# First attention chunk: probabilities' sums on GpSimd, scores issued two heads ahead, later weight splits and key preparation

## The chip, the cores and the metric

The kernel runs on one core of one Trainium2 chip. The metric is the device time of one execution in microseconds (us). The engines are named as in the profile: PE multiplies matrices, PEld is its weight load, DVE is VectorE, ACT is ScalarE, POOL is GpSimd, SP is SyncE, which here only issues transfers. PSUM is the memory that PE writes its results to, SBUF the one that holds everything else.

## The reference

Three parts follow each other, all in fp32.

```python
# 1. attention, q k v: (2, 8, 576, 64), f: (2, 8, 576)
scores = scale * np.matmul(q, k.transpose(0, 1, 3, 2))
cum = np.cumsum(np.log(np.clip(f, 0.0001, 1.0)), axis=-1)
scores = np.where(causal, -1000000000.0, scores + cum[..., :, None] - cum[..., None, :])
attn = np.exp(scores - np.max(scores, axis=-1, keepdims=True))
x = np.matmul(attn / (np.sum(attn, axis=-1, keepdims=True) + 1e-09), v)
# 2. four experts on all 1152 tokens, x: (1152, 512), w1: (4, 512, 1024), w2: (4, 1024, 512)
p = domain_probs / (domain_probs.sum(-1, keepdims=True) + 1e-09)
for e in range(E):
    out += p[:, e:e + 1] * (np.maximum(x @ w1[e], 0.0) @ w2[e])
# 3. an MLP: 512 -> 2048 -> 512
h = out @ w_in
y = (h * (1.0 / (1.0 + np.exp(-1.702 * h)))) @ w_out
```

## The kernel before

**Precision.** Each fp32 operand is held as a rounded part (`hi`: `whi`, `xh`, `qhi`) and a remainder (`lo`: `wlo`, `xl`, `qlo`); a product is three matmuls, hi·hi, lo·hi and hi·lo. So weights, keys, queries and activations each need one rounding instruction and one subtraction. For a weight tile the rounding is on ACT (L72) and the subtraction `wlo` on DVE or POOL (L250). For a pair of heads the keys `ks` are rounded on ACT and their remainders subtracted on DVE for one head and on POOL for the other (L579); the queries are rounded (L69) and subtracted (L597) on POOL.

**Chunks.** Tokens go through attention in chunks. The first is batch 0, queries 0 to 255, one head at a time for eight heads; later ones take two heads at a time. When the chunk's attention output exists, the first layer of the first expert starts on it.

**The first chunk.** `first_step(i)` issues step i of twelve; `in_turn` ties the instructions of the steps to the written order on PE, DVE, ACT and POOL. For head h the stages are: scores on PE (L660) into PSUM; mask and maximum on DVE (L690); exponential and sum on ACT (L706); sum plus 1e-9 and reciprocal on DVE (L713, L714); normalisation on POOL (L716); transposes on PE (L818); a copy to SBUF (`first_copy`, L828, on DVE, that of head 7 on ACT); per pair of heads the product with the values on PE (`emit_pv`, L772), then `xh` on ACT and `xl` on DVE (L783, `emit_x2`). `emit_first(k)` (L979) is the first layer for the 128 features that head pair k yields: 4 groups g of 3 matmuls. `turn(FILL[i])` issues dummy matmuls of 128x512 (L1199) whose result nobody reads. Beside that the steps issue the splits of the first weights ("a" from step 2, "b" from step 6, one tile a step, four tiles each), and the keys and queries of the next pair of heads (steps 7 and 9).

**After the first chunk** a scheduler that simulates the engines places the rest: attention of the later chunks between units of the first layer (L958) and of the second (L1127; its results leave PSUM on DVE by `acc`, L1169 and L1171, which needs the probabilities `dpn`). Loads all go through SP's queue in one order (L78), and a load that overwrites a buffer waits in that queue for the buffer's last reader.

**Probabilities.** The table `dpraw` is loaded third; six DVE instructions make `dpn` of it (L461 to L466), ahead of the first maximum:

```python
        tc.keep_in_program_order(nc.vector.tensor_add(s, v[:, 0], v[:, 1]))
        for e in (2, 3):
            nc.vector.tensor_add(s, s, v[:, e])
        nc.vector.tensor_scalar(out=s, in0=s, scalar1=1e-9, scalar2=None, op0=ALU.add)
        nc.vector.reciprocal(out=s, in_=s)
        nc.vector.tensor_mul(out, v, s.unsqueeze(1).to_broadcast([128, 4, NTILE]))
```

Of the kernel before, what the change touches and what calls it, by code (L numbers as in the profile page):

```python
# [18 lines left out]
SA = 256  # L19
# [14 lines left out]
NTILE = NT // 128  # L34
NBLK = 12
NMOE = 8
WARM, FILL = 11, (4, 3, 3, 2, 2, 2, 3, 3,)


class Halves:  # L40
# [11 lines left out]
def attn_moe_mlp(ctx: ExitStack, tc: tile.TileContext, qk0, qk1, qk2, v0, vp, fg, dp, wa_moe, wb_moe, wa_mlp, wb_mlp, out):  # L52
# [176 lines left out]
    def split_w(kind, v_, g):  # L229
        while (kind, v_, g) not in raw_w:  # L230
            next(cv_gen[0])
            load_owed()
        raw = raw_w.pop((kind, v_, g))
        p = wa_p if kind == "a" else wb_p
        if kind == "b" and v_ in (v_exp, v_exp + 2):
            hi, lo = (t[:, g].rearrange("p (a c) -> p a c", a=4) for t in tsr)
        else:
            hi = p.tile([128, 4, 128], F32R, tag="hi", name="whi")
            lo = p.tile([128, 4, 128], F32R, tag="lo", name="wlo")
        hf = hi.rearrange("p a c -> p (a c)")  # L240
        lf = lo.rearrange("p a c -> p (a c)")
        round_act(hf, raw)
        (wa if kind == "a" else wb)[v_, g] = (hi, lo)
        if kind == "a" and v_ in joint:
            joint_raw[g] = raw

        def rest():
            while pair_due:
                pair_due.pop()()
            (nc.gpsimd if v_ == 0 and kind == 'a' and g < 4 else nc.vector).tensor_sub(lf, raw, f(hf))  # L250
            if g % 2:
                if kind == "a" and v_ in joint and v_ not in placed:
                    sum_weights(v_, g // 2)
                pair_due.append(load_pair)

        lo_due.append(rest)
        lo_of.append((kind, v_, g))
# [195 lines left out]
        load(raw, dp)  # L453
        return raw

    def make_probabilities(raw):

        out = const.tile([128, 4, NTILE], F32, name="dpn")
        s = const.tile([128, NTILE], F32, name="dps")
        v = raw.rearrange("p (j e) -> p e j", e=4)  # L460
        tc.keep_in_program_order(nc.vector.tensor_add(s, v[:, 0], v[:, 1]))  # L461
        for e in (2, 3):
            nc.vector.tensor_add(s, s, v[:, e])
        nc.vector.tensor_scalar(out=s, in0=s, scalar1=1e-9, scalar2=None, op0=ALU.add)
        nc.vector.reciprocal(out=s, in_=s)
        nc.vector.tensor_mul(out, v, s.unsqueeze(1).to_broadcast([128, 4, NTILE]))  # L466
        return out

    def begin_late():
        att_scope.close()  # L470
# [69 lines left out]
    def load_plain_late():  # L540
        for i in (1, 0):
            load(groups[4][i][0:64], qk0[1, 1 - i].rearrange("d (g s) -> d g s", g=4))
        load_plain_values(0)
        load_pair()
        load_pair()
        load_plain_values(4)

    def load_heads(p, h0):
# [79 lines left out]
    def emit_scores(c, u):  # L628
# [4 lines left out]
        for q0 in tiles:  # L633
# [13 lines left out]
            for a, z, _ in mm:  # L647
                if plain(c):
                    if q0 == 0:
                        bank = ps_s.tile([128, 512], F32, tag="s", name="s")  # L650
                    pts.append(bank[:, q0:q0 + w])
                else:
                    if not both or not pts:
                        bank = ps_s.tile([128, 512], F32, tag="s", name="s")
                    pts.append(bank[:, 256:256 + w] if both and pts else bank)
                out.append((q0, w, a, z, pts[-1]))
# [163 lines left out]
    def first_copy(h):  # L820

        pt = first_t.pop(h)
        ph = pt_p.tile([128, 4, SB], F32, tag="ph", name="ph").rearrange("p i q -> p (i q)")
        ph_of[0, h] = [ph[:, :SA], ph[:, SA:SA + 128]]
        if h == 7:
            round_act(ph[:, :SA + 128], pt[:, :SA + 128])
        else:
            nc.vector.tensor_copy(ph[:, :SA + 128], pt[:, :SA + 128])  # L828

    def first_step(i):  # L830

        n = len(first_seq)
        p, h0 = passes[1], 0
        prep = [(7, lambda: prep_keys(p, h0, 0)), (7, lambda: prep_keys(p, h0, 1)), (9, lambda: prep_keys(p, h0, 2)),
                (9, lambda: prep_queries(p, h0, 1, (0,))), (9, lambda: prep_queries(p, h0, 1, (1,)))]
        for j in (0, 1) if i == 0 else (i + 1,):
            if j < n:
                emit_scores(*first_seq[j])
        if 3 <= i < n + 3:
            emit_pv(0, i - 3)  # L840
        if i >= 7 and x_used[0] < x_made[0] and x_used[0] < 3:
            emit_first(x_used[0])
            x_used[0] += 1
        if i < n:
            emit_max(*first_seq[i])
            emit_exp(*first_seq[i])
        if 1 <= i <= n:
            emit_norm(*first_seq[i - 1])
        if 2 <= i < n + 2:
            first_copy(i - 2)  # L850
        if 3 <= i < n + 3:
            emit_x2(0, i - 3)
        split_rest()
        for kind, p0 in (("a", 2), ("b", 6)):
            if 0 <= i - p0 < 4:
                split_w(kind, 0, i - p0)
                pass
        for j, fn in prep:
            if i == j:
                fn()  # L860
        if i < len(FILL):
            turn(FILL[i])
        if 1 <= i <= n:
            first_tr(i - 1)
        if i == 0:
            load_cum(p, h0)
        if i == 8:
            load_heads(passes[1], 2)
        if i == 9:
            load_values(p, h0)  # L870

    def attention():
# [16 lines left out]
        for i in range(len(seq) + L_X2 + 1):  # L889
            done = None  # L890
            new = [k for k in nxt if first[k] == i + LEAD]
            new_q = [k for k, j in first_q.items() if j == i + LEAD]
            last_pool = [j for j in nc.cur_bb.bb.instructions if j.engine == nc.gpsimd.engine][-1]
            with tc.issue_after(last_pool) if i == 0 else ExitStack():
                for k in new:
                    prep_parts(*k)
                for k in new_q:
                    prep_queries(*k)
            for k in [k for k in nxt if first[k] == i + 2]:
# [65 lines left out]

    first_p = []

    def emit_first(k, last=False):

        v_, b, c = units[0]  # L970
        for g in range(4):
            if k == 0:
                if g % 2 == 0:
                    first_p.append(ps_tile())
            po = first_p[g // 2][:, SA * (g % 2):SA * (g % 2) + SA]
            whi, wlo = wa[v_, g]
            for j, (w, x) in enumerate([(whi, xh), (wlo, xh), (whi, xl)]):

                nc.tensor.matmul(po, lhsT=w[:, k, :], rhs=x[c][:, k, :],  # L979
                                 start=(k == 0 and j == 0 and g % 2 == 0), stop=(k == 3 and j == 2 and g % 2 == 1))  # L980
# [250 lines left out]
            load_plain_late()  # L1231
    nc.vector.tensor_scalar(out=fr, in0=cum, scalar1=1.0 / NEG, scalar2=None, op0=ALU.mult)
    nc.scalar.dma_start(out=cumd, in_=fr)
    dpn = make_probabilities(dp_raw)
    load_heads(passes[1], 0)
    for _ in range(2):
        load_pair()
# [15 lines left out]
        while ready[0] < c:  # L1253
            pull()

    x_used = [0]
    for i in range(len(first_seq) + 4):
        in_turn(first_step, i)
    ready[0] = 0

    pin_from = [None, 0]
# [115 lines left out]
    late_by = [3]  # L1377
    rest_gen, rest_from = [], seq.index((1,) + units[6])
    cv_due = [0]
    in_turn(emit_first, 3, True)  # L1380
    for i, (kind, v_, b, c) in enumerate(seq):
        if kind == 1 and c < NCH:
            drain(c)
# [161 lines left out]
```

## Time and profile before

| what | value |
|---|---|
| time, median of 3 runs (lowest, highest) | 687.27 us (686.98, 688.13) |
| time of the profiled execution | 687.52 us |
| its span, first to last instruction | 685.8 us |
| PE busy | 676.4 us |
| DVE busy | 531.0 us |
| ACT busy | 353.6 us |
| POOL busy | 244.7 us |
| mean granted TensorE clock | 0.999 |

The profile is of one execution. Its own time is 1.7 us more than its span, which is what lies outside the first and the last instruction. Starts in the rows below are counted from the start of the span. A row with "x4" stands for four instructions one behind another, its second number for the time from the start of the first to the end of the last. What stands in square brackets at a row's end is idle time ahead of it and what ended that.

### The profile page before, as it was taken

Reading aid. Unit: us, or ns where it says so; the run is one execution under the profiler, and the core shown is the slowest. Engines: PE = TensorE matmul, PEld = TensorE weight load, DVE = VectorE, ACT = ScalarE, POOL = GpSimd, SP = SyncE. Lnnn points to the kernel's source line nnn. Section 1 sums busy time; section 2 is a strip of 40 time slices with the busy share of each in tenths; the row PEclk is TensorE's granted clock in tenths of the full one; section 3 lists DMA queues with packets and bytes.
Section 4 is the critical chain, followed back from the end, with each engine's and each line's share of the span. In section 5 each row is a group of like instructions: output and inputs, shape, how many; then the busy total and the mean of one; then the engine's idle time right before and its main releaser. Section 6 shows DMA issues by size and latency. Waiting matters only on the chain.

```text
span 685.8 us, 11068 instructions
## 1 busy us (share of the span) xinstructions
PE 676.4 (99%) x3921; PEld 596.8 (87%) x3921; DVE 531.0 (77%) x1097; ACT 353.6 (52%) x821; POOL 244.7 (36%) x302
## 2 busy tenths in 40 slices
PE   8998999999999999999999999999999999999997
PEld 4797889889888898898898898898999998998986
DVE  6896767788698778777987879767799989988532
ACT  5768767667633735635336253362447453552420
POOL 6886577463342454543135324132003300120000
PEclk9999999999999999999999999999999999999999
DMA  8796637145232135053531423413332534441012
GB/s 254 232 307 245 232 114 246 27 151 169 93 123 92 38 117 169 32 159 133 170 108 48 153 77 108 127 41 100 119 108 77 168 124 153 141 153 62 1 46 93
DMA packets 41063, 87.59 MB, mean 128 GB/s; under 512 B 3720, under 2 KB 5776, under 8 KB 40752
## 3 DMA queue, kind: packets, MB, share of 16 engines
q1 hardware_dynamic: 40680, 84.75, 38.0%
q0 software_dynamic: 288, 2.10, 0.8%
q8 instruction: 31, 0.51, 0.3%
q14 instruction: 24, 0.20, 0.1%
q10 hardware_dynamic: 40, 0.04, 0.0%
HBM read 73.98 MB, written 12.88 MB: 127 GB/s over the span
## 4 chain that ended last, share of the span: by engine, by line
PE 90%; DVE 4%; POOL 2%; DMA 1%; ACT 1%; issue 1%; SPq 0%; POOLq 0%; DVEq 0%
PE m L1127 41%; PE m L1002 23%; PE m L958 15%; PE s L660 4%; PE x L772 3%; PE t L734 3%; DMA qr<-in_qk_dram 1%; POOL e L716 1%; PE m L1283 1%; DMA dpraw<-in_dp_dram 1%; POOL qlo L597 1%; POOL qhi L69 1%; DVE acc L1171 0%; POOL ks L579 0%; DVE wf L434 0%
## 5 line engine op out<-in xcount | busy, mean ns | idle before, releaser
L1127 PE MATMUL m<-whi,hh 128*128 128x512 f32 x392 | 109.6, 393 | 0.0
L1127 PE MATMUL m<-wlo,hh 128*128 128x512 f32 x392 | 108.3, 391 | 0.0
L1127 PE MATMUL m<-whi,hl 128*128 128x512 f32 x392 | 108.2, 390 | 0.0
L250 DVE TENSOR_TENSOR wlo<-wst,whi 128x512 fp32r<-128x512 f32 x132 | 101.5, 783 | 6.3 <-ACT whi L72 5.8
L1013 POOL TENSOR_TENSOR hl<-jc,hh 128x320 fp32r<-128x320 f32 (+1 forms) x60 | 53.1, 888 | 141.1 <-ACT hh L72 141.0
L72 ACT ACTIVATE whi<-wst 128x512 fp32r<-128x512 f32 x136 | 80.6, 624 | 26.3 <-PE m L1127 14.2
L1127 PEld LDWEIGHTS m<-wlo,hh 128*128 128x128 f32 x392 | 73.3, 188 | 15.5
L1127 PEld LDWEIGHTS m<-whi,hl 128*128 128x128 f32 x392 | 73.4, 188 | 15.2
L1127 PEld LDWEIGHTS m<-whi,hh 128*128 128x128 f32 x392 | 71.9, 188 | 12.5
L271 POOL TENSOR_TENSOR sr<-wst 128x256 f32<-128x256 f32 x20 | 18.1, 903 | 149.4 <-DMA wst<-wm 79.6
L716 POOL TENSOR_SCALAR e<-e,sm 128x128 f32<-128x128 f32 (+4 forms) x72 | 44.9, 636 | 48.3 <-DVE sm L714 31.7
L1011 ACT ACTIVATE jc<-jc 128x320 f32<-128x320 f32 (+1 forms) x60 | 27.1, 451 | 54.6 <-DVE jc L1008 54.2
L1171 DVE SCALAR_TENSOR_TENSOR acc<-m,dpn,acc 128x512 f32<-128x512 f32 x63 | 46.5, 744 | 7.8 <-PE m L1127 7.6
L958 PE MATMUL m<-xh,whi 128*128 128x256 f32 (+2 forms) x256 | 51.1, 315 | 0.3 <-ACT xh L72 0.3
L958 PE MATMUL m<-xh,wlo 128*128 128x256 f32 (+2 forms) x256 | 50.6, 313 | 0.0
L958 PE MATMUL m<-xl,whi 128*128 128x256 f32 (+2 forms) x256 | 50.5, 314 | 0.0
L706 ACT ACTIVATE e<-e,mx 128x128 f32<-128x128 f32 (+4 forms) x72 | 41.7, 581 | 10.3 <-DVE mx L690 9.9
L958 PEld LDWEIGHTS m<-xh,whi 128*128 128x128 f32 x256 | 41.2, 189 | 2.2 <-ACT xh L72 0.6
L1110 ACT ACTIVATE m<-m 128x384 f32<-128x384 f32 x48 | 23.0, 479 | 37.1 <-DVE m L1008 35.5
L958 PEld LDWEIGHTS m<-xh,wlo 128*128 128x128 f32 x256 | 41.3, 189 | 0.8
L958 PEld LDWEIGHTS m<-xl,whi 128*128 128x128 f32 x256 | 41.0, 189 | 0.6
L1040 ACT ACTIVATE u<-m 128x320 f32<-128x320 f32 (+2 forms) x26 | 11.2, 432 | 50.5 <-PE m L1002 50.5
(174 smaller groups left out, 1510.1 us busy)
## 6 DMA issues: line engine op xcount, KB each, us to landing
wst<-in_wa_moe_dram SPq DMA_DIRECT2D x28, 512.0 KB, 4.2
wst<-in_wb_moe_dram SPq DMA_DIRECT2D x28, 512.0 KB, 4.3
mst<-in_wa_mlp_dram SPq DMA_DIRECT2D x16, 512.0 KB, 3.7
wm<-wf SPq DMA_DIRECT2D x32, 256.0 KB, 4.0
mst<-in_wb_mlp_dram SPq DMA_DIRECT2D x16, 512.0 KB, 4.2
wst<-wm SPq DMA_DIRECT2D x16, 512.0 KB, 3.9
cb<-cumd SPq DMA_DIRECT2D x16, 256.0 KB, 4.4
qr<-in_qk_dram SPq DMA_DIRECT2D x8, 384.0 KB, 4.6
```

The costliest lines, as they stand in the source:

```text
L72: return nc.scalar.activation(out=out, in_=in_, func=AF.Copy)
L250: (nc.gpsimd if v_ == 0 and kind == 'a' and g < 4 else nc.vector).tensor_sub(lf, raw, f(hf))
L660: nc.tensor.matmul(pt[:, :z - a], lhsT=lr[i][0], rhs=lr[i][1], start=i == 0 and not (both and pt is not bank), stop=i == n - 1, skip_group ...
L706: nc.scalar.activation(out=e[:, off:off + w], in_=e[:, off:off + w], func=AF.Exp, scale=-1.0, bias=mx, accum_out=sm[:, 0, k:k + 1])
L716: nc.gpsimd.tensor_scalar(out=e[:, off:off + w], in0=e[:, off:off + w], scalar1=sm[:, 0, i:i + 1], scalar2=1.0, op0=ALU.mult, op1=ALU.mult)
L958: nc.tensor.matmul(p[:, :n], lhsT=w[:, k, :], rhs=x[c][:, k, :], start=(j == 0 and k == 0), stop=(j == 2 and k == 3))
L1002: nc.tensor.matmul(p[:, :WN], lhsT=w[a][:, k, :], rhs=x[z][:, k, :], start=start and j == 0 and k == 0, stop=stop and j == 2 and k == 1, s ...
L1011: nc.scalar.activation(out=r, in_=r, func=AF.Relu)
L1013: nc.gpsimd.tensor_sub(hl[:, g, :], r, f(hh[:, g, :]))
L1110: nc.scalar.activation(out=p[:, :n], in_=p[:, :n], func=AF.Gelu_apprx_sigmoid)
L1127: nc.tensor.matmul(p, lhsT=h_tile(v_, b, c, j, x, k), rhs=wb[v_, k][w].rearrange("p a c -> p (a c)"), start=i == 0 and k == 0, stop=i == 2 ...
L1171: nc.vector.scalar_tensor_tensor(out=a, in0=p, scalar=d, in1=a, op0=ALU.mult, op1=ALU.add)
```

## The change

All of it is in the code of the first chunk and of what is issued beside it:

- The probabilities' three additions and the 1e-9 go to POOL in step 2, the reciprocal and the product stay on DVE, in step 10.
- Scores are issued two heads ahead instead of one (three heads in step 0), with a third PSUM bank, taken from the pool of the later matmuls. In a step the product with the values comes first, then the transposes, then the scores; the transposes of a head move from the end of one step to the start of the next.
- 11 dummy matmuls instead of 22.
- The weights "a" are split a step later, "b" two steps later; three of the four `wlo` of "a" are on POOL, before all four.
- The copy of head 7 goes from ACT to DVE. The keys and queries of the next pair come in steps 8 and 9. The `emit_first` of pairs 0 to 2 keep a fixed table; the fourth group of each is issued last.
- The rounding of the second pair's keys on ACT is ordered behind the last ACT instruction of the first chunk. On SP two weight loads go ahead of a load of values.

```diff
-WARM, FILL = 11, (4, 3, 3, 2, 2, 2, 3, 3,)
+WARM, FILL = 11, (1, 2, 2, 2, 1, 2, 1)
+X2_AT = {5: 1, 7: 3, 9: 5, 10: 7}
...
-            (nc.gpsimd if v_ == 0 and kind == 'a' and g < 4 else nc.vector).tensor_sub(lf, raw, f(hf))
+            (nc.gpsimd if v_ == 0 and kind == 'a' and g < 3 else nc.vector).tensor_sub(lf, raw, f(hf))
...
+    def sum_probabilities():
+
+        v = dp_raw.rearrange("p (j e) -> p e j", e=4)
+        nc.gpsimd.tensor_add(p_sum, v[:, 0], v[:, 1])
         for e in (2, 3):
...
+            nc.gpsimd.tensor_add(p_sum, p_sum, v[:, e])
+        nc.gpsimd.tensor_scalar(out=p_sum, in0=p_sum, scalar1=1.0, scalar2=1e-9, op0=ALU.mult, op1=ALU.add)
+
+    def make_probabilities():
+
+        nc.vector.reciprocal(out=p_sum, in_=p_sum)
+        nc.vector.tensor_mul(dpn, dp_raw.rearrange("p (j e) -> p e j", e=4), p_sum.unsqueeze(1).to_broadcast([128, 4, NTILE]))
...
-        load_plain_values(0)
         load_pair()
         load_pair()
+        load_plain_values(0)
         load_plain_values(4)
...
-                        bank = ps_s.tile([128, 512], F32, tag="s", name="s")
+                        bank = ps_tile() if hs[0] % 3 == 2 else ps_s.tile([128, 512], F32, tag="s", name="s")
...
-        if h == 7:
-            round_act(ph[:, :SA + 128], pt[:, :SA + 128])
-        else:
-            nc.vector.tensor_copy(ph[:, :SA + 128], pt[:, :SA + 128])
+        nc.vector.tensor_copy(ph[:, :SA + 128], pt[:, :SA + 128])
...
-        prep = [(7, lambda: prep_keys(p, h0, 0)), (7, lambda: prep_keys(p, h0, 1)), (9, lambda: prep_keys(p, h0, 2)),
+        prep = [(8, lambda: prep_keys(p, h0, 0)), (9, lambda: prep_keys(p, h0, 1)), (9, lambda: prep_keys(p, h0, 2)),
                 (9, lambda: prep_queries(p, h0, 1, (0,))), (9, lambda: prep_queries(p, h0, 1, (1,)))]
-        for j in (0, 1) if i == 0 else (i + 1,):
+        if 3 <= i < n + 3:
+            emit_pv(0, i - 3)
+        if 2 <= i < n + 2:
+            first_tr(i - 2)
+        for j in range(3) if i == 0 else (i + 2,):
             if j < n:
                 emit_scores(*first_seq[j])
-        if 3 <= i < n + 3:
-            emit_pv(0, i - 3)
-        if i >= 7 and x_used[0] < x_made[0] and x_used[0] < 3:
-            emit_first(x_used[0])
-            x_used[0] += 1
+        for k, gs in {7: [(0, range(3))], 8: [(1, (0, 1))], 9: [(1, (2,))],
+                      10: [(2, range(3)), (0, (3,)), (1, (3,)), (2, (3,))]}.get(i, ()):
+            emit_first(k, gs)
...
-        if 3 <= i < n + 3:
-            emit_x2(0, i - 3)
-        split_rest()
-        for kind, p0 in (("a", 2), ("b", 6)):
-            if 0 <= i - p0 < 4:
-                split_w(kind, 0, i - p0)
-                pass
+        if i in X2_AT:
+            emit_x2(0, X2_AT[i])
+        if i == 2:
+            sum_probabilities()
+        if i == 10:
+            make_probabilities()
         for j, fn in prep:
             if i == j:
                 fn()
+        if i != 7:
+            split_rest()
+        for kind, p0 in (("a", 3), ("b", 8)):
+            if 0 <= i - p0 < 4:
+                split_w(kind, 0, i - p0)
         if i < len(FILL):
             turn(FILL[i])
-        if 1 <= i <= n:
-            first_tr(i - 1)
...
+                for j in nc.cur_bb.bb.instructions[begin:]:
+                    if i == 0 and j.engine == nc.scalar.engine:
+                        keep_order([first_act[0], j])
...
-    dpn = make_probabilities(dp_raw)
...
+    first_act = [j for j in nc.cur_bb.bb.instructions if j.engine == nc.scalar.engine][-1:]
...
-    in_turn(emit_first, 3, True)
+    in_turn(emit_first, 3, range(4), True)
```

Lines of the changed kernel are a few higher than those of before for the same code: L660 is L663, L690 is L693, L713 is L716, L772 is L775, L818 is L821, L250 is L251, L579 is L582, L1169 is L1177, L1199 is L1207. Three places show how instructions move.

PE's order at the first product with the values (`x<-ph,v`), in steps 2 and 3, before (`t` are transposes, `s` scores, `m<-acc_79` a dummy):

```order
L818 MATMUL t<-identr,e 128x128 x3
L660 MATMUL s<-acc_79 128x128
L660 MATMUL s<-acc_79 128x256
L772 MATMUL x<-ph,v_157 64x256 x2
L772 MATMUL x<-ph,v_157 64x128 x2
L1199 LDWEIGHTS acc_79
L1199 MATMUL m<-acc_79 128x512
```

and with the change:

```order
L775 MATMUL x<-ph,v_158 64x256 x2
L775 MATMUL x<-ph,v_158 64x128 x2
L821 MATMUL t<-identr,e 128x128 x3
L663 MATMUL s<-acc_79 128x128
L663 MATMUL s<-acc_79 128x256
L1207 LDWEIGHTS acc_79
L1207 MATMUL m<-acc_79 128x512
```

The product with the values went from behind the scores to ahead of the transposes and of the scores.

DVE's order from the last heads of the first chunk to the first maximum of the next chunk (`e,mx<-s,cb`), before (`ph` is a copy of transposed probabilities, `dpn` the experts' probabilities, `dps` their sum):

```order
L828 COPY ph<-t 128x384
L250 TENSOR_TENSOR wlo<-wst,whi 128x512
L579 TENSOR_TENSOR ks<-kq,ks 64x576
L713 TENSOR_SCALAR sm<-sm 128x1 x2
L714 RECIPROCAL sm<-sm 128x2
L828 COPY ph<-t 128x384
L783 TENSOR_TENSOR xl<-x,xh 128x256
L250 TENSOR_TENSOR wlo<-wst,whi 128x512 x2
L579 TENSOR_TENSOR ks<-kq,ks 64x576
L783 TENSOR_TENSOR xl<-x,xh 128x256
L250 TENSOR_TENSOR wlo<-wst,whi 128x512
L690 ISA e,mx<-s,cb 128x384
```

and with the change:

```order
L828 COPY ph<-t 128x384
L251 TENSOR_TENSOR wlo<-wst,whi 128x512
L828 COPY ph<-t 128x384
L786 TENSOR_TENSOR xl<-x,xh 128x256
L582 TENSOR_TENSOR ks<-kq,ks 64x576
L251 TENSOR_TENSOR wlo<-wst,whi 128x512
L786 TENSOR_TENSOR xl<-x,xh 128x256
L469 RECIPROCAL dps<-dps 128x9
L470 TENSOR_TENSOR dpn<-dpraw,dps 128x36
L251 TENSOR_TENSOR wlo<-wst,whi 128x512 x3
L582 TENSOR_TENSOR ks<-kq,ks 64x576
L693 ISA e,mx<-s,cb 128x384
```

Three of the weights' subtractions now stand in a row behind the two instructions on the probabilities, and behind the copy of the head before the last seven subtractions (five `wlo`, two `ks`) stand ahead of that maximum.

DVE's order between the two maxima of the next chunk's 288-wide parts (`e,mx<-s,cbs` and `e,mx<-s,cbs,mx`), before:

```order
L690 ISA e,mx<-s,cbs 128x288
L690 ISA mx 128x1
L713 TENSOR_SCALAR sm<-sm 128x1 x3
L714 RECIPROCAL sm<-sm 128x2 x2
L250 TENSOR_TENSOR wlo<-wst,whi 128x512
L690 ISA e,mx<-s,cbs,mx 128x288
L690 ISA mx 128x1
```

and with the change:

```order
L693 ISA e,mx<-s,cbs 128x288
L693 ISA mx 128x1
L716 TENSOR_SCALAR sm<-sm 128x1
L1177 TENSOR_SCALAR acc_79<-m,dpn 128x512
L717 RECIPROCAL sm<-sm 128x2
L251 TENSOR_TENSOR wlo<-wst,whi 128x512
L1177 TENSOR_SCALAR acc_79<-m,dpn 128x512
L251 TENSOR_TENSOR wlo<-wst,whi 128x512 x3
L693 ISA e,mx<-s,cbs,mx 128x288
L693 ISA mx 128x1
```

The second of these maxima went behind two results of the second layer (`acc`) and four `wlo`, where one `wlo` stood.

## Rows read from the trace of the kernel before

**Rows 1.** Windows: stretch, length; busy PE, PEld, DVE, ACT, POOL; clock, DMA, GB/s

```profile
0.00:34.00 34.00, 30.59 (x181) 20.23 (x182) 25.88 (x93) 22.48 (x59) 25.12 (x41) 1.00 0.77 244
34.00:130.00 96.00, 94.05 (x672) 81.99 (x671) 71.08 (x203) 67.48 (x179) 62.78 (x83) 1.00 0.60 205
```

**Rows 2.** Waits of PE, 30 to 130 us: total, times, longest

```profile
PE t L734 <- POOL e L716: 1.4, 1, 1.4
PE s L660 <- DVE mx L690: 0.5, 1, 0.5
PE s L660 <- POOL qlo L597: 0.3, 1, 0.3
```

**Rows 3.** Chain up to 34 us: start us, us, what

```profile
2.50 3.79 DMA dpraw<-in_dp_dram
...
6.95 1.10 DVE dps L464
...
8.46 0.28 DVE e L690
...
22.17 1.43 PE m L979 x12
```

**Rows 4.** Timeline of PE at 6 us: start us, us, instruction

```profile
6.37 1.55 PE L660 MATMUL s<-raw 65*128 65x128 f32 x8
```

**Rows 5.** Timeline of POOL: start us, us, instruction

```profile
10.34 1.74 POOL L716 TENSOR_SCALAR e<-e,sm 128x128 f32<-128x128 f32 x4 [1.83 <-DVE sm L714]
...
14.39 1.27 POOL L250 TENSOR_TENSOR wlo<-wst,whi 128x512 fp32r<-128x512 f32 x1
...
25.71 0.82 POOL L716 TENSOR_SCALAR e<-e,sm 128x128 f32<-128x128 f32 x2 [1.43 <-PE x L772]
26.61 1.75 POOL L579 TENSOR_TENSOR ks<-kq,ks 64x576 fp32r<-64x576 f32 x1
28.45 1.15 POOL L69 TENSOR_SCALAR qhi<-qr 128x768 fp32r<-128x768 f32 x1
29.69 2.80 POOL L597 TENSOR_TENSOR qlo<-qr,qhi 64x384 fp32r<-64x384 f32 x2
...
35.44 2.74 POOL L597 TENSOR_TENSOR qlo<-qr,qhi 64x384 fp32r<-64x384 f32 x2
```

**Rows 6.** Timeline of DVE, 25 to 37 us

```profile
25.43 0.54 DVE L828 COPY ph<-t 128x384 f32<-128x384 f32 x1
26.04 0.42 DVE L783 TENSOR_TENSOR xl<-x,xh 128x256 fp32r<-128x256 f32 x1
26.38 2.54 DVE L250 TENSOR_TENSOR wlo<-wst,whi 128x512 fp32r<-128x512 f32 x2
28.94 1.26 DVE L579 TENSOR_TENSOR ks<-kq,ks 64x576 fp32r<-64x576 f32 x1
...
30.58 1.04 DVE L250 TENSOR_TENSOR wlo<-wst,whi 128x512 fp32r<-128x512 f32 x1
31.61 0.56 DVE L690 CUSTOM_DVE_ANT_0 e<-s,cb 128x384 f32<-128x384 f32 x1
...
32.44 0.69 DVE L250 TENSOR_TENSOR wlo<-wst,whi 128x512 fp32r<-128x512 f32 x1 [0.27 <-ACT whi L72]
...
34.73 2.57 DVE L250 TENSOR_TENSOR wlo<-wst,whi 128x512 fp32r<-128x512 f32 x2
```

**Rows 7.** Timeline of PE, 28 to 34 us

```profile
28.90 0.87 PE L772 MATMUL x<-ph,v 128*64 128x256 f32 x8
...
32.82 0.39 PE L660 MATMUL s<-ks,qhi 128*128 128x512 f32 x1
...
33.40 0.62 PE L1127 MATMUL m<-whi,hh 128*128 128x512 f32 x2
```

**Rows 8.** Timeline of SP's queue at 41 us

```profile
41.02 1.09 SPq L78 DMA_DIRECT2D cbs<-cumd  x2
```

**Rows 9.** Waits of ACT, 40 to 55 us: total, times, longest

```profile
ACT whi L72 <- DMA wst<-in_wa_moe_dram: 3.8, 1, 3.8
```

More of the change, by code (lines that the diff above doesn't have):

```diff
@@ L454, in load_probabilities @@
         return raw
[L456 to L461, printed above, removed]
-        for e in (2, 3):
[L463 to L467, printed above, removed]
+    p_sum = const.tile([128, NTILE], F32, name="dps")
+    def sum_probabilities():
+        v = dp_raw.rearrange("p (j e) -> p e j", e=4)
+        nc.gpsimd.tensor_add(p_sum, v[:, 0], v[:, 1])
+        for e in (2, 3):
+            nc.gpsimd.tensor_add(p_sum, p_sum, v[:, e])
[3 more added lines that the diff above has]
+        nc.vector.tensor_mul(dpn, dp_raw.rearrange("p (j e) -> p e j", e=4), p_sum.unsqueeze(1).to_broadcast([128, 4, NTILE]))
     def begin_late():
@@ L893, in attention @@
             last_pool = [j for j in nc.cur_bb.bb.instructions if j.engine == nc.gpsimd.engine][-1]
+            begin = len(nc.cur_bb.bb.instructions)
             with tc.issue_after(last_pool) if i == 0 else ExitStack():
@@ L966, in attn_moe_mlp, with emit_first @@
     first_p = []
-    def emit_first(k, last=False):
+    def emit_first(k, gs=range(4), last=False):
         v_, b, c = units[0]
-        for g in range(4):
+        for g in gs:
             if k == 0:
@@ L1254, in drain @@
             pull()
-    x_used = [0]
+    dpn = const.tile([128, 4, NTILE], F32, name="dpn")
     for i in range(len(first_seq) + 4):
         in_turn(first_step, i)
+    first_act = [j for j in nc.cur_bb.bb.instructions if j.engine == nc.scalar.engine][-1:]
     ready[0] = 0
```

## Prediction, made before the changed kernel ran

> **What bounds the kernel now.** I read the windows first: from 34 to 130 us PE is busy in 94.05 of 96 us, from 0 to 34 in 30.59, at a granted clock of 1.00 in both [rows 1]. So a change pays only where PE waits or does work that nobody needs, and that lies in the first 34 us, where part of the busy time is dummy matmuls. PE's waits behind them are few: between 30 and 130 us 0.5 on a maximum of DVE, 1.4 on a normalisation of POOL and 0.3 on `qlo` [rows 2]. The chain of what ended last shows what sets the first stage, the first chunk's head pipeline: the probabilities' table lands at 6.29, DVE's work on it (one addition of 1.10 among it) ends just ahead of the first maximum at 8.46 [rows 3], and then PE, ACT, DVE and POOL take turns. POOL's timeline shows the pipeline's length: the first head's normalisation starts at 10.34, the last head's at 25.71, with four weight subtractions of 1.27 between, and behind them come keys and queries almost without a gap [rows 5]. PE makes the next chunk's scores meanwhile; the score for its second unit starts at 32.82 [rows 7], and that is the point at which I compare.
>
> **The head stage: what the change saves.** (1) The first maximum no longer stands behind the six instructions on the probabilities. What it needs otherwise is the first head's scores, and they are half of a row that lasts from 6.37 to 7.92 [rows 4]. So it starts at about 7.2 to 7.3, 1.2 us earlier. The three additions and the 1e-9 now run on POOL between the normalisations of heads 1 and 2, and no row shows a POOL instruction on nine columns. Their cost is between 0 (POOL idle there) and 1.7 us, four at the 0.43 that heads 0 and 1 need for one on up to 256 columns (1.74 for 4 [rows 5]); I take 1.4, since the time of a small instruction falls less than its columns. (2) Heads 0 and 1 are normalised from 9.1 to 10.9, head 2 from about 12.3, behind the sums, head 3, for which DVE's sum is ready only then, from 13.7. From there POOL sets the pitch: a normalisation (0.82) and a subtraction (1.27) [rows 5] are 2.09 a head, three times, which gives head 6 at 20.0 and head 7 at about 21.3, against 25.71. That is 4.4 us. The last pair's product with the values follows DVE's copies: head 6 is normalised up to 20.8, transposed behind PE's other work and copied from about 22.2 to 22.7; then `wlo` a3 takes 1.2 and head 7's copy 0.54 [rows 6], so both are there at 24.4, and behind the `emit_first` of that step PE starts the product at about 25.0, against 28.90 [rows 7]. (3) Behind it PE has the same work as before up to the second unit's score, 32.82 − 28.90 = 3.92 less the 0.35 on `qlo`, which is now ready, plus 18 matmuls of `emit_first` that were ahead of it before, at 0.12 each (1.43 for 12 [rows 3]), so 2.15. PE would stand at that score at 25.0 + 3.57 + 2.15 + 0.3 for a late `xl`, that is at 31.0. By then it has also done two matmuls of the second layer (0.46 from 33.40 to 33.86 [rows 7]) that came behind the score before. Equal work is thus reached at 32.82 + 0.46 = 33.28, and **PE would be 2.3 us ahead, if nothing else is late**.
>
> **What is late next: DVE.** PE's score for the second unit needs a PSUM bank that the next chunk's first maximum frees; that maximum stood at 31.61 [rows 6] and PE needed it only later. In the new order seven subtractions of two SBUF inputs (five `wlo`, two `ks`), one copy, two `xl`, the reciprocal and the product stand between the copy of head 6 and that maximum, and POOL runs its own keys and queries beside them, starting when head 7 is normalised. How dear the seven are is the disputed price. The rows bound it. One took 0.69 (32.44), started in a gap of POOL's. Under POOL's run from 26.61 to 38.18, seven of the same kind took 2.54 (two), 1.26, 1.04, 0.69 and 2.57 (two), 8.10 together, 1.16 each [rows 6]. Their ends fall about 0.55 behind the ends of POOL's instructions: 28.92 behind POOL's 28.36, 30.20 behind 29.60 [rows 5, 6]. So a subtraction on DVE waits for the POOL instruction under way and then runs.
>
> The Trainium skill says the same as a rule ("SBUF — State Buffer", section "Who interferes with whom"): a DVE instruction with two SBUF inputs and a GpSimd instruction that reads SBUF exclude each other for a whole instruction, and who issues first goes first. The trace agrees in the ends named above; it differs in the price, since turns taken strictly would make every subtraction as dear as the POOL instruction ahead of it, and some here ran back to back.
>
> Sum by the rows: 22.7 (end of head 6's copy) + 8.1 (seven at 1.16) + 0.54 (copy of head 7) + 0.8 (two `xl` at 0.42) + 0.4 for reciprocal and product (8.46 − 6.95 − 1.10 [rows 3]) = 32.6 for the maximum; the product with two SBUF inputs may wait once more, 0.5. The maximum takes 0.56 [rows 6], so the score starts at 33.2 to 33.7 instead of at equal work's 33.28: **−0.1 to +0.4 us, and the 2.3 are spent**. With the seven at 0.7 the maximum is at about 29.5, PE does not wait, and the 2.3 stay. I take the price under a busy POOL, since POOL's eight instructions start at about 22.1 and DVE's seven at 22.7, the situation of the rows from 26.61 on.
>
> **Other parts.** The 11 dummies that go filled waits of PE for the pipeline; what they take is in the times of (2), and PE's clock stayed at 1.00 in this stage with its few gaps, so I price their lack at nothing. Scores two heads ahead, the transposes' place and the third bank are what lets PE keep step with POOL's 2.09; their own cost is nothing, since the same instructions are issued. The `wlo` that goes from POOL to DVE (1.27 on POOL) is in both sums above. ACT loses one copy. `v` of the first heads behind two weight loads lands before PE's first product with it, at about 15 us; if it did not, that product would be late by a transfer's share, no more than 1 us, inside a stage that DVE gives back anyway.
>
> **Later loads.** The second 288-wide maximum now stands behind two `acc` (put at 0.7 each, as an uncovered subtraction on as many elements) and three more `wlo` of 0.7 to 1.2 each, and comes at 44 to 46. Before, SP's queue issued the next `cbs` at 41.02 [rows 8], right behind that maximum, since the transfer overwrites what it reads; the weight load and the queries behind it go 3.5 to 5 us later. ACT already waited 3.8 us for that weight load [rows 9], with PE going on; a later load costs PE something only past the slack that PE's 1.95 us of idle time in 34 to 130 us [rows 1] shows. The order from about 130 us on is the same. I put this at 0, with ends of −1.9 (the waits of 0.5 and 1.4 [rows 2] vanish, as POOL and DVE are ahead) and +2.
>
> **Sum.** Against the profiled execution's own 687.52 (0.25 above the median of the runs, 687.27; 1.7 of it lie outside the span): −0.1 to +0.4 for the handover, 0 for the rest, gives 687.4 to 687.9 as an execution and, with the 0.25 taken off, 687.2 to 687.7. I say **687.3**.
>
> **The rivals.**
> *DVE is not held (faster).* If POOL and DVE fall into a rhythm in which DVE's subtractions run between POOL's, or POOL is late, the seven cost 0.7 to 0.9, the maximum comes at 29.5 to 31, PE keeps 2 to 2.3 us, and some of the later waits fall too: 687.3 − 2.3 = 685.0, from 684 to 685.9. For it: PE's own lead of 2.3 is worked from many agreeing rows, and one of the seven rows is 0.69. Against: six of them are not. Chance 0.31.
> *Strict turns (slower).* If each of DVE's seven waits for one of POOL's eight instructions, the eight take what they took, 38.18 − 26.61 = 11.57 [rows 5], from 22.1 on, to 33.7; a last subtraction ends at 34.3, the maximum at 34.9, and the score starts 1.6 us behind equal work: 688.9, and with the later loads up to 689.7. It decides from the point where a subtraction costs over 1.3 on the mean. For it: the pairs at 2.54 and 2.57 are at 1.27 and 1.28. Against: the others are below. Chance 0.19.
> The rule of the Trainium skill named above, taken alone, is this case: every two-input subtraction would wait for a whole POOL instruction.
> *Late loads (slower).* The handover costs nothing, but the weights behind SP's wait come too late for PE: up to +2, 689. Chance 0.06; others that cost more (a bank, the ACT order) 0.04.
> *The change does nothing there.* Were the pitch set by DVE or PE instead of POOL, the last head would come no sooner, and the sum would be 0 as well; it is in the forecast's share.
>
> **How the numbers follow.** The forecast, no change that shows, has 0.40; about 0.2%, 1.4 us, is what a measurement of this kernel can tell from no change, so it covers 686.0 to 688.6. Faster has 0.31, slower 0.29 (0.19, 0.06, 0.04). The forecast alone spans 686.3 to 688.3. For 8 in 10 the range takes most of both neighbours: down to 684.2, where the gain is kept and part of the later waits goes, up to 689.7, where turns are strict and loads late.
>
> **What would show it.** The first maximum at 7.2 to 7.3; POOL's normalisation of the last head at 21 to 22; the last product with the values at about 25; the seven subtractions at about 1.16 each; the first maximum of the next chunk at 32 to 33, with PE waiting for it; the second 288-wide maximum at 44 to 46 and SP's wait with it. If the subtractions are at 0.7 to 0.9, the forecast is wrong toward 685; if PE waits for DVE past 34, or shows waits on weights before 130 us, toward 689.

## The result and the profile after

The changed kernel is slower: 694.08 us (692.92 to 694.52, 4 runs) against 687.7 (686.98 to 688.73), ratio 1.0089, 95% interval 1.0069 to 1.0109. That is outside the range of the prediction. The profiled execution took 692.92, its span is 691.2, 5.4 more than before. It was the shortest of the four: its mean granted clock was 0.997, that of the other three, which took 693.73 to 694.52, was 0.995.

The windows show where the first loss lies, from 34 to 41 us (stretch, its length, busy PE, PEld, DVE, ACT, POOL, clock, DMA share, GB/s), first before, then after:

```profile
34.00:41.00 7.00, 7.00 (x38) 5.81 (x37) 7.00 (x21) 5.42 (x14) 5.00 (x7) 1.00 0.95 274
```

```profile
34.00:41.00 7.00, 5.87 (x20) 4.83 (x21) 6.61 (x19) 2.70 (x7) 0.26 (x2) 0.76 1.03 351
```

Here the granted clock is 0.76 on the mean, where it was 1.00; its two levels are 1.2 and 2.4 GHz, so 7 us at 0.24 less are at most 1.7 us of work. PE's waits between 30 and 130 us (total, times, longest), where before there were 0.5 on a maximum, 1.4 on a normalisation and 0.3 on `qlo` [rows 2], are now one line:

```profile
PE s L663 <- DVE mx L693: 5.0, 4, 3.7
```

PE's timeline has the longest of these waits, 3.7, ahead of the second unit's score:

```profile
25.16 0.86 PE L775 MATMUL x<-ph,v 128*64 128x256 f32 x6 [0.51 <-DVE ph L828]
...
30.75 0.73 PE L1135 MATMUL m<-whi,hh 128*128 128x512 f32 x2
35.13 0.80 PE L663 MATMUL s<-ks,qhi 128*128 128x512 f32 x1 [3.65 <-DVE mx L693]
```

Most of the last pair's product with the values starts at 25.16, where it started at 28.90 [rows 7], and PE has done all that lies ahead of the score, the two matmuls `m<-whi,hh` too, at 31.5. The kernel before had done the same work at 33.28, so PE is 1.8 ahead. Then it stands until 35.13, which is 1.85 behind. DVE's timeline shows why:

```profile
8.07 0.29 DVE L693 CUSTOM_DVE_ANT_0 e<-s,raw 128x128 f32<-128x128 f32 x1 [2.49 <-PE s L663]
...
23.19 1.45 DVE L251 TENSOR_TENSOR wlo<-wst,whi 128x512 fp32r<-128x512 f32 x1
24.56 0.54 DVE L828 COPY ph<-t 128x384 f32<-128x384 f32 x1
...
25.47 1.55 DVE L582 TENSOR_TENSOR ks<-kq,ks 64x576 fp32r<-64x576 f32 x1
27.05 1.40 DVE L251 TENSOR_TENSOR wlo<-wst,whi 128x512 fp32r<-128x512 f32 x1
...
28.93 0.25 DVE L470 TENSOR_TENSOR dpn<-dpraw,dps 128x36 f32<-128x36 f32 x1
29.11 3.91 DVE L251 TENSOR_TENSOR wlo<-wst,whi 128x512 fp32r<-128x512 f32 x3
33.05 1.43 DVE L582 TENSOR_TENSOR ks<-kq,ks 64x576 fp32r<-64x576 f32 x1
34.51 0.56 DVE L693 CUSTOM_DVE_ANT_0 e<-s,cb 128x384 f32<-128x384 f32 x1
...
34.99 0.69 DVE L251 TENSOR_TENSOR wlo<-wst,whi 128x512 fp32r<-128x512 f32 x1
```

The seven subtractions from 23.19 to 34.48 take 1.45, 1.55, 1.40, 3.91 for three, and 1.43: 9.74, or 1.39 each, against 1.16 in [rows 6]. Beside them POOL runs the instructions of [rows 5] without a gap:

```profile
20.82 1.75 POOL L719 TENSOR_SCALAR e<-e,sm 128x128 f32<-128x128 f32 x4
22.65 1.43 POOL L582 TENSOR_TENSOR ks<-kq,ks 64x576 fp32r<-64x576 f32 x1
24.18 1.15 POOL L70 TENSOR_SCALAR qhi<-qr 128x768 fp32r<-128x768 f32 x1
25.41 2.49 POOL L600 TENSOR_TENSOR qlo<-qr,qhi 64x384 fp32r<-64x384 f32 x2
27.99 1.15 POOL L70 TENSOR_SCALAR qhi<-qr 128x768 fp32r<-128x768 f32 x1
29.22 1.84 POOL L582 TENSOR_TENSOR ks<-kq,ks 64x576 fp32r<-64x576 f32 x1
31.12 2.74 POOL L600 TENSOR_TENSOR qlo<-qr,qhi 64x384 fp32r<-64x384 f32 x2
```

DVE's ends follow POOL's ends by 0.5 to 0.6: `wlo` at 28.45 behind the two `qlo` at 27.90, `ks` at 34.48 behind the last `qlo` at 33.86. What reads PSUM is not held: the copy of head 7 took 0.54. So every subtraction waited for one POOL instruction, and the maximum came at 34.51 instead of 31.61 [rows 6].

For the later part the same matmuls in both kernels are compared, first before, then after:

```profile
196.68 0.88 PE L958 MATMUL m<-xh,whi 128*128 128x384 f32 x4
```

```profile
200.12 0.88 PE L966 MATMUL m<-xh,whi 128*128 128x384 f32 x4
```

The difference is 3.44 us there: 1.85 of the score and 1.6 that PE lost behind it, while the clock was low. Of the 5.4 us some 2 come still later: compared matmul by matmul, PE is 3.4 late up to 212 us, 4.5 from 230 and 5.2 from 345. PE's waits from 200 to 345 us, where the kernel before has none:

```profile
PE m L1010 <- DVE jc L1016: 0.7, 1, 0.7
PE m L1010 <- ACT th L73: 0.5, 1, 0.5
```

### The profile page after: what moved, and what is told of

Its sections match the earlier page's. It is cut to its first block, busy times and chain, and to the rows that moved or that the text cites. A ratio compares the mean times of both kernels' runs of the same rounds, so it can differ in the third digit from the quotient of the medians.

```text
span 691.2 us, 11042 instructions
## 1 busy us (share of the span) xinstructions
PE 677.8 (98%) x3909; PEld 598.1 (87%) x3910; DVE 535.1 (77%) x1095; ACT 353.3 (51%) x820; POOL 243.0 (35%) x305
## 4 chain that ended last, share of the span: by engine, by line
PE 87%; DVE 7%; DMA 2%; issue 1%; ACT 1%; SPq 0%; POOL 0%; DVEq 0%
PE m L1135 40%; PE m L1010 22%; PE m L966 15%; PE s L663 4%; PE x L775 3%; PE t L737 3%; DVE wlo L251 2%; DMA cb<-cumd 1%; DVE tr L332 1%; DMA wst<-in_wa_moe_dram 1%; DVE hl L1124 1%; PE m L1291 1%; DVE ks L582 1%; DVE acc L1179 0%; DVE wf L435 0%
## 5 line engine op out<-in xcount | busy, mean ns | idle before, releaser
L251 DVE TENSOR_TENSOR wlo<-wst,whi 128x512 fp32r<-128x512 f32 x133 | 104.6, 802 | 2.6 <-ACT whi L73 2.3
```

Source lines behind the costliest of these rows:

```text
L251: (nc.gpsimd if v_ == 0 and kind == 'a' and g < 3 else nc.vector).tensor_sub(lf, raw, f(hf))
```

## The experiments

Ratios are to the kernel before, run on the same chip. Times are medians.

| run | edit | us | ratio (95%) | next chunk's first maximum | clock, 34 to 41 us |
|---|---|---|---|---|---|
| changed kernel | | 694.08 | 1.0089 (1.0069 to 1.0109) | 34.51 | 0.76 |
| e1_dummies | dummies in the wait | 695.6 | 1.0103 (1.0078 to 1.0129) | 35.29 | 0.76 |
| e2_b6 | "b" split at 6 to 9 | 693.03 | 1.0073 (1.0047 to 1.0100) | 35.10 | 0.98 (0.50 from 30 to 34) |
| e3_act_round | queries rounded on ACT | 692.49 | 1.0062 (1.0040 to 1.0084) | 33.22 | 0.76 |
| e4_noql | no queries' remainders | 689.59 | 1.0024 (1.0014 to 1.0035) | 32.54 | 1.00 |
| e5_prob | before, probabilities alone | 688.86 | 1.0008 (0.9996 to 1.0019) | 31.90 | 1.00 |
| e6_lateb | three `wlo` behind the maximum | 689.62 | 1.0022 (1.0011 to 1.0033) | 31.07 | 1.00 |
| e7_cbs3 | third buffer for cbs | 693.61 | 1.0083 (1.0067 to 1.0099) | 34.61 | 0.76 |
| e8_both | e6 and e7 | 691.93 | 1.0064 (1.0044 to 1.0083) | 30.63 | 1.00 |
| e9_nocount | bank without the counter | 692.55 | 1.0067 (1.0052 to 1.0082) | 34.50 | 0.54 |
| e10_late_nocount | e6 and e9 | 688.74 | 1.0012 (1.0002 to 1.0021) | 31.52 | 1.00 |
| e11_late_act | e3, e6 and e9 | 688.06 | 1.0006 (0.9996 to 1.0016) | 31.38 | 1.00 |
| e12_late4_act | e11, four `wlo` of "a" on POOL | 687.32 | 0.9989 (0.9979 to 0.9998) | 29.17 | 1.00 |

**The port: e3_act_round and e4_noql.** The theory is that DVE's subtractions and POOL's instructions exclude each other (the expectations call it a port that is held in turns); the rival is that DVE is slow there for another reason.

```diff
-            round_pool(st["qs", c][0], raw)
+            (round_act if p is passes[1] and h0 < 4 else round_pool)(st["qs", c][0], raw)
```

> The changed kernel with the rounding of the queries of the first two pairs of heads on ACT instead of POOL: two of POOL's eight instructions beside DVE's seven subtractions are gone, the work is the same. Theory (a), a port that DVE and POOL hold in turns: the first maximum comes 1.5 to 2.3 us earlier (32.2 to 33), PE's wait falls to 1.3 to 2.2, and the time to 689 to 691. Rival (b), DVE is slow there for another reason (loads into SBUF, its own pipeline): the maximum stays within 0.5 of 34.5 and the time at 693 to 694.

```diff
-            nc.gpsimd.tensor_sub(l, r, h)
+            if not (p is passes[1] and h0 < 4 and c == 1):
+                nc.gpsimd.tensor_sub(l, r, h)
```

> The changed kernel without the subtraction that makes the queries' remainders of the first two pairs of heads (four POOL instructions of 1.2 to 1.4 left out; the remainder used is then zero). DVE's order up to the first maximum is unchanged. Theory (a), the shared port: POOL's run beside DVE's seven subtractions is 5.7 us instead of 11.2, four of them stay at 1.2 to 1.5 and three fall to 0.6 to 0.7, so the maximum comes at 31.5 to 32.5, PE waits under 1.5, the clock stays at 1.00, and the time falls to 688 to 690. Rival (b): the subtractions cost 1.39 without POOL beside them; then nothing moves by more than 0.5.

DVE's timeline of the kernel without remainders:

```profile
23.70 1.44 DVE L251 TENSOR_TENSOR wlo<-wst,whi 128x512 fp32r<-128x512 f32 x1
...
25.97 0.75 DVE L582 TENSOR_TENSOR ks<-kq,ks 64x576 fp32r<-64x576 f32 x1
26.75 1.21 DVE L251 TENSOR_TENSOR wlo<-wst,whi 128x512 fp32r<-128x512 f32 x1
...
28.59 3.13 DVE L251 TENSOR_TENSOR wlo<-wst,whi 128x512 fp32r<-128x512 f32 x3
31.75 0.75 DVE L582 TENSOR_TENSOR ks<-kq,ks 64x576 fp32r<-64x576 f32 x1
32.54 0.56 DVE L694 CUSTOM_DVE_ANT_0 e<-s,cb 128x384 f32<-128x384 f32 x1
```

The order on DVE is the same, and the seven take 7.28, 1.04 each, instead of 1.39; the one at 25.97 ran free in 0.75 and the last in 0.75. The maximum came at 32.54, at the end of what was expected, and the time fell to 689.59. With two of POOL's instructions gone it came at 33.22, 1.3 earlier, a little short of the 1.5 to 2.3. The rival is out.

The time of e3 fell less than expected. One reason is the clock, which the two runs show together (next part). The other is a wait of PE for rounded weights at 53 to 55 us, behind a load that ACT waited for (3.1 us in e3, 3.3 in e4); the changed kernel has no such wait. First e3, then e4, in its profiled execution, which was the longest of its ten:

```profile
PE m L966 <- ACT whi L73: 1.5, 1, 1.5
```

```profile
PE m L967 <- ACT whi L73: 2.2, 1, 2.2
```

**The clock: e3 against e4, and e1.** Two matmuls that follow each other in both kernels, the second unit's score and a later group of the second layer, and the windows from 34 to 41; first e3, then e4:

```profile
33.84 0.50 PE L663 MATMUL s<-ks,qhi 128*128 128x512 f32 x1 [2.23 <-DVE mx L693]
...
38.51 1.09 PE L1135 MATMUL m<-whi,hh 128*128 128x512 f32 x4
```

```profile
34.00:41.00 7.00, 7.00 (x26) 5.66 (x27) 5.70 (x18) 2.95 (x9) 1.38 (x3) 0.76 1.03 307
```

```profile
33.16 0.50 PE L664 MATMUL s<-ks,qhi 128*128 128x512 f32 x1 [1.00 <-DVE mx L694]
...
36.27 1.07 PE L1136 MATMUL m<-whi,hh 128*128 128x512 f32 x4
```

```profile
34.00:41.00 7.00, 7.00 (x39) 5.98 (x38) 6.65 (x20) 4.01 (x11) 2.06 (x3) 1.00 1.04 339
```

The score is 0.68 later in e3, the group behind it 2.24. The work between is the same, so 1.6 us were lost to the clock, after PE had waited 2.2 in e3 and 1.0 in e4. This part of the loss no step of the prediction had. In the changed kernel it is the 1.6 above, and in e9 it was more:

```profile
34.00:41.00 7.00, 5.88 (x16) 4.74 (x17) 6.63 (x19) 2.27 (x7) 0.07 (x1) 0.54 1.04 316
```

The executions of one kernel say the same. In the changed kernel, e1, e2, e3 and e7 the mean granted clock of an execution is either 0.995 to 0.996 or 0.997 to 0.998, and in each of the five every execution at the lower one took longer than every one at the higher; the means differ by 0.8 to 2.0 us. So the 6.4 us between the medians, where the profiled executions differ by 5.4, go with a lower clock in three of the four.

The direct test did not work:

```diff
     in_turn(emit_first, 3, range(4), True)
+    turn(14)
```

> The changed kernel with 14 dummy matmuls (some 3.0 us at 0.216 each) behind the last emit_first, where PE waits 3.65 us for the next chunk's first maximum. Theory (a): the wait itself costs about 1.8 us and the granted clock that falls to half behind it, for 3.4 us, another 1.7; then the dummies keep the clock at 1.00, PE's wait shrinks to about 1, and the time falls by 1.5 to 2 us, to about 692. Rival (b): the fall of the clock costs nothing, since DVE is what PE waits for in that stretch too; then the time stays at 694 within 0.5 or rises.

The dummies stood where PE waits, but the scheduler placed what follows in another order:

```profile
31.14 3.19 PE L1207 MATMUL m<-acc 128*128 128x512 bf16 x14
...
37.12 1.62 PE L1135 MATMUL m<-whi,hh 128*128 128x512 f32 x4 [0.36 <-DVE hl L997]
```

PE still waited 1.4 and 0.4 behind them, the clock fell all the same (the matmuls at 37.12 are slow again), and another wait, 1.3 on weights, came before 65 us. 695.6 says nothing for or against the clock's price.

**The later split: e2_b6.**

```diff
-        for kind, p0 in (("a", 3), ("b", 8)):
+        for kind, p0 in (("a", 3), ("b", 6)):
```

> The changed kernel with the weights b split at steps 6 to 9 again, as before. Theory (a): seven subtractions of two SBUF inputs stand between the copy of head 6 and the next chunk's first maximum, whatever their order, each held for a POOL instruction (1.39 on the mean in the changed kernel); the undo leaves seven there, so the maximum stays at 34 to 35, and the time at 692 to 695. Rival (b): the later split is what piles the subtractions up ahead of that maximum; then it comes at about 31, as before the change, and the time falls to 687 or less.

The maximum came at 35.10 and the time was 693.03. Three `wlo`, 4.46 us for the three, now stood ahead of head 7's copy, and PE waited there:

```profile
PE x L775 <- DVE ph L828: 3.5, 1, 3.5
```

Behind that wait the clock was at 0.50 from 28 to 34 us. So the later split alone is not the cause: without it PE meets held subtractions, and the clock behind the wait, at an earlier place. But the maximum at 35.10 is not theory (a)'s: POOL stood idle for 2.1 us of that stretch, waiting for a load of queries; three of the four subtractions left ran in 0.68 to 0.75 each; and the maximum waited 1.14 for PE's score and not for DVE's queue. The number was right by luck.

**Part of the subtractions behind the maximum: e6_lateb.** The b weights 1 to 3 are split after the first chunk, and each `wlo` is ordered behind the maximum.

```diff
+            if v_ == 0 and kind == "b" and g:
+                keep_order([next_max[0], ins.ins])
```

> The changed kernel with three of the b weights' subtractions queued behind the next chunk's first maximum instead of ahead of it: four held subtractions are left there instead of seven. Theory (a): the maximum comes three times 1.3 earlier, at about 30.5, PE's wait of 3.65 goes, the clock stays at 1.00, and PE passes 36 us with a lead of 1 to 2 us on the kernel before; behind it the late weight load (some 2 us at 60, which the wait hides in the changed kernel) and two waits of 1.0 and 0.7 at about 215 and 340 come out, so 687 to 690. Rival (b), the lead is given back in the first stage whatever DVE does: 692 or more.

```profile
29.83 1.31 DVE L472 TENSOR_TENSOR dpn<-dpraw,dps 128x36 f32<-128x36 f32 x1
31.07 0.54 DVE L695 CUSTOM_DVE_ANT_0 e<-s,cb 128x384 f32<-128x384 f32 x1
...
31.54 3.76 DVE L251 TENSOR_TENSOR wlo<-wst,whi 128x512 fp32r<-128x512 f32 x4
```

The maximum came at 31.07, and the clock stayed (1.00 from 34 to 41). PE's wait ahead of the second unit's score fell from 3.65 to 0.89, and 4.5 of the 6.4 us are gone. The lead was not kept whole: the product for `dpn`, 0.25 in the changed kernel, was now held itself (1.31), and the four `wlo` stand ahead of the second maximum.

**One part alone: e5_prob.** The kernel before with only the probabilities moved.

> The kernel of before with one part of the change alone: the probabilities' sums on POOL in step 2, reciprocal and product on DVE in step 10. Theory (a), the loss is made behind the heads, by DVE's queue: this part alone starts the first maximum at 8.0 to 8.1 (where the changed kernel has it) and gives 0 to -0.5 us, so 687.1 to 687.7. Rival (b), the sums on POOL are part of the loss: 688.5 or more.

The first maximum came at 7.61, earlier than expected. The median, 688.86, lies in the range of (b), but the interval of the ratio holds 1: no change can be told. A gain of more than 0.3 us is excluded, a loss of up to 1.3 is not. In the profiled execution the last pair's product started 0.8 earlier than before, yet the matmul compared above came at 198.06, 1.4 later than before, with PE waiting 2.1 for maxima and 0.8 for weights between 30 and 130 us. So a share of this part in the loss is neither shown nor ruled out.

**Late loads: e7_cbs3 and e8_both.**

```diff
-    kq_p = pool("kq", 3, scope=att_scope)
+    kq_p = pool("kq", 2, scope=att_scope)
-    cbs_p = pool("cbs", 2, scope=att_scope)
+    cbs_p = pool("cbs", 3, scope=att_scope)
```

> The changed kernel with a third buffer for cbs (and two instead of three for the keys, which pays for its room): the load of cbs no longer waits for the late 288-wide maximum, so the weight load behind it in SP's queue goes some 7 us earlier. Theory (a): in the changed kernel PE is 3.4 us late already when it comes to these weights, so their lateness costs nothing on top; 693.5 to 694.5, no change. Rival (b), the late load is part of the 6.4 us: 691.5 to 692.5.

> Both edits: the subtractions behind the maximum and the third buffer for cbs. Theory (a): with PE's wait gone the late weight load is the next limit, so this is 1 to 2 us faster than the kernel with the late subtractions alone, at 686 to 688.5, what is left over 685 being the waits at about 215 and 340. Rival (b), the load is not on the path: the same time as that kernel within 0.5.

SP's queue in the changed kernel and in e7 (the load of `cbs`, and behind it the weights):

```profile
48.62 1.09 SPq L79 DMA_DIRECT2D cbs<-cumd  x2
49.81 0.54 SPq L79 DMA_DIRECT2D wst<-in_wa_moe_dram  x1
```

```profile
41.01 1.09 SPq L79 DMA_DIRECT2D cbs<-cumd  x2
42.20 0.53 SPq L79 DMA_DIRECT2D wst<-in_wa_moe_dram  x1
```

The weights went 7.6 us earlier and the time did not move beyond its noise. This alone does not show that their lateness cost nothing, since the buffer taken from the keys may have cost what the weights gained: the next keys were loaded at 52.30 instead of 50.91, and the compared matmul came at 201.16, 1.0 later than in the changed kernel. What shows it is the one line of PE's waits above: from 30 to 130 us the changed kernel's PE waits for maxima and for no weights. e8 does not tell whether they would be next: it is slower than e6, where it was expected faster. With two buffers for keys, the next keys were loaded later (49.24, in e6 46.06). That pair of edits can't be read. But e3 and e4, whose PE is less late, wait 1.5 and 2.2 for weights (above).

**The waits behind 200 us: e9_nocount.** `ps_tile` counts its calls, and in the late stage the count modulo 8 decides from which of two pools a PSUM tile comes. The third bank for scores makes two such calls. The edit takes the bank without them. From 190 us to the end, 2688 matmuls, PE's order in the trace of e9 is that of the kernel before; in the changed kernel only the last 240 agree.

```diff
-                        bank = ps_tile() if hs[0] % 3 == 2 else ps_s.tile([128, 512], F32, tag="s", name="s")
+                        bank = ps_m.tile([128, 512], F32, tag="m", name="m") if hs[0] % 3 == 2 else ps_s.tile(...)
```

> The changed kernel with one thing else: the third bank for scores is taken from the same three PSUM buffers, but without moving the counter that later deals the results of matmuls between two sets of PSUM buffers. By that counter alone the order of all engines from about 215 us on is again that of the kernel before. Theory (a): the lateness of 3.4 us at 36 to 200 us stays, the 1.1 at about 218 and the 0.7 at about 340 go, so 692 to 692.8. Rival (b): those later waits come from late loads or from chance, not from the order; then 694 within 0.5.

```profile
201.48 0.88 PE L966 MATMUL m<-xh,whi 128*128 128x384 f32 x4
```

In its profiled execution the lateness at the compared matmul is 4.80 (the clock was low for longer), and that of the whole span is 4.8 too: 690.6 against 685.8. Nothing is lost behind it, where the changed kernel lost 2 (5.4 − 3.4). The waits on `jc` and `th` are gone, and the median fell by 1.5. The two intervals of the ratio overlap, but executions with the same mean clock of 0.995 took 693.73 to 694.52 in the changed kernel and 692.33 to 693.27 here.

**A version of all: e10 to e12.**

> The same, and three of the b weights' subtractions behind the next chunk's first maximum, as in the run that gave 689.6. Theory (a): the two edits add up; PE passes 36 us at +0.7 with the clock at 1.00, and the 1.2 to 1.8 behind 200 us are gone: 687.4 to 688.4, within 0.2% of the kernel before. Rival (b): 689 to 690.

> The same again, and the queries' rounding of the first two pairs on ACT instead of POOL, which takes two of POOL's instructions from beside DVE's subtractions. Theory (a): the first maximum comes some 1 us earlier than in the kernel without this edit (30 instead of 31), PE keeps 0.5 to 1.5 us more of its lead, 686.5 to 687.7: the first version that is not slower than the kernel before, perhaps faster. Rival (b): ACT's rounding of the weights comes later by the two instructions (1.7 us) and PE waits there instead; 688.5 or more.

> The same with the fourth subtraction of the a weights on POOL again, as before the change: one held subtraction less on DVE, one instruction of 1.27 more on POOL ahead of keys and queries. Theory (a), the port is used by turns and the sum of both engines' instructions counts: the first maximum moves by less than 0.7 either way and the time stays within 0.5 of the run without it. Rival (b), DVE's queue alone counts: 1.3 us earlier, 685.5 to 686.5.

e10 came at 688.74, 0.9 under e6 where 1.2 to 2.2 were expected; PE waited for `v` in it, the load that the change puts behind two weight loads:

```profile
PE x L779 <- DMA v<-in_v_dram: 0.9, 1, 0.9
```

e11's median is 0.7 lower still, at 688.06 (the intervals overlap), but its maximum moved by 0.1 only; so the reason given for it did not hold. e12's maximum came at 29.17, 2.2 earlier, against both expectations (under 0.7, or 1.3), and its 687.32 lies between them. Of the 2.2, 1.2 were there at the copy of head 6, at 22.19 against 23.35 in e11, where PE had waited 0.6 for `v`; from that copy on it is 1.0, which lies between the two as well. The fourth `wlo` on POOL ran while DVE copied from PSUM, which POOL doesn't hold. POOL's row first, then DVE's:

```profile
22.00 1.30 POOL L251 TENSOR_TENSOR wlo<-wst,whi 128x512 fp32r<-128x512 f32 x1
```

```profile
22.19 0.56 DVE L832 COPY ph<-t 128x384 f32<-128x384 f32 x1 [1.14 <-PE t L825]
23.23 0.56 DVE L832 COPY ph<-t 128x384 f32<-128x384 f32 x1 [0.48 <-PE t L825]
...
29.17 0.54 DVE L695 CUSTOM_DVE_ANT_0 e<-s,cb 128x384 f32<-128x384 f32 x1
```

e12 is the fastest version; its 0.9989 is a gain of 0.1% on the kernel before, with an interval that just leaves out 1.

## Why the prediction was wrong

- **The head stage** was right in size. The last pair's product started at 25.16 (25.0 forecast), the lead at the score was 1.8 to the end of the matmuls ahead of it (2.3 forecast). The first maximum, though, came at 8.07, not at 7.2 to 7.3: DVE waited for scores there. POOL's four small instructions took 1.07 (1.4 taken), and the last head was normalised at 21.7 (21.3).
- **The step that failed** is "Sum by the rows: 22.7 ... + 8.1 (seven at 1.16)". The place, the queue and the mechanism were as told; the seven cost 9.74. The mean of 1.16 was taken over rows among which one was free and others ran among instructions that read PSUM; in a row, with POOL never idle, each waited its turn. The maximum was 1.9 later than the 32.6 of the sum: 1.6 by the seven, 0.5 by the copy of head 6, which ended at 23.19 and not at 22.7, less 0.2 on the rest. The "strict turns" rival had the maximum at 34.3 to 34.9 and 1.6 us of loss; measured were 34.51 and 1.85. It had a chance of 0.19. The Trainium skill's rule ("SBUF — State Buffer", section "Who interferes with whom") that the engine that comes second is blocked for the whole instruction is what the trace shows here, and the prediction had priced it too low. By this alone the time would have been about 689.1 (687.27 + 1.85), still inside the range; it left the range by the two terms that follow, which the prediction had put at nothing.
- **What no step had**: the wait cost twice. PE's clock fell behind it, 1.6 us in the profiled execution, more in that of e9. The Trainium skill tells of such a case, an engine that waits in the middle of a kernel and resumes at the lower clock ("TensorE: Matmul & The Clock Gate", section "HAM oscillation — how this bites in real kernels"); the windows at 0.76 and 0.54 agree. "PE's clock stayed at 1.00 in this stage with its few gaps" was true of the dummies that went, and not of the gap that the forecast itself put there.
- **"The order from about 130 us on is the same"** was wrong: a counter that the third bank moves set another order from about 215 us on, which cost 2 us in the profiled execution; without it the median of e9 was 1.5 lower.
- **Late loads** at no cost was right for the changed kernel, but in part by luck: its PE was late already, and where it was less late, in e3 and e4, it waited 1.5 and 2.2 for weights. The maximum that the loads wait for came at 48.09, not 44 to 46. `v` was in time in the changed kernel's profiled execution; in those of e1, e7, e10 and e11 PE waited 0.6 to 1.0 for it. The probabilities' part gave no gain that can be measured.
- Open: the exact price of the clock in the median, since the one direct test changed the order; whether the late weights would limit the changed kernel with its lead kept (e8 can't tell); and the 1.2 us that e6 and e10 to e12 lost between 100 and 205 us, with a wait of PE of 1.3 on a copy of ACT, which was not tried.

## What to carry to other kernels

A lead that one stage gains is worth only what the engine behind it can follow: price the next engine's queue in the order that the change makes, and price instructions of two engines that hold each other up by full turns when they stand in a row beside a busy partner. A forecast wait of PE of some microseconds can have a second price, the clock after it: here a wait of 2.2 us cost 1.6 more, one of 1.0 nothing. And compare the order of the whole program, not only of the stage that was edited: a counted pool or a rotating buffer can move work far behind it.

## What was not expected of the hardware

Seven subtractions on DVE took 1.39 each beside POOL, where one with POOL idle took 0.69, while copies from PSUM of 128x384 took 0.54 to 0.56 either way. And the low clock lasted unequally after the same wait: 0.76 on the mean from 34 to 41 us in the changed kernel, 0.54 in e9, with PE waiting 3.7 for the same maximum in both.
